# Half-head attention visits, a split last query chunk and a cross-chunk background order in a four-layer attention kernel

## The chip, the cores and the metric

One NeuronCore of a Trainium2 chip runs the whole program. The metric is the device time in microseconds (us) of one execution, from launch to the last output byte. Times of single instructions come from one profiled execution; its clock counts from the first instruction of the span.

The engines are named as in the profile: PE is TensorE (matmuls), PEld its weight loads, ACT is ScalarE (exponentials), DVE is VectorE, POOL is GpSimd, SP is SyncE, which issues the DMAs.

## The reference

Four layers, A, B, A, B, each a residual block around a layer norm. S is 2048 rows, D is 1024, 32 heads of 32. Layers 0 and 2 are linear attention with softmax features, layers 1 and 3 are full softmax attention (no mask).

```python
def _A_ref(x, wqkv, w_phi, wo):
    ...
    pq = jnp.einsum("bhsd,hdf->bhsf", q, w_phi)
    pk = jnp.einsum("bhsd,hdf->bhsf", k, w_phi)
    phi_q = jnp.concatenate([_softmax(pq, axis=-1), _softmax(-pq, axis=-1)], axis=-1)
    phi_k = jnp.concatenate([_softmax(pk, axis=-1), _softmax(-pk, axis=-1)], axis=-1)
    kv = jnp.einsum("bhsf,bhsd->bhfd", phi_k, v)
    z  = jnp.einsum("bhsf->bhf", phi_k)
    num = jnp.einsum("bhqf,bhfd->bhqd", phi_q, kv)
    den = jnp.einsum("bhqf,bhf->bhq", phi_q, z)[..., None] + 1e-6
    o = num / den
    return (lambda x, *d: x.transpose(*d))(o, 0, 2, 1, 3).reshape(B, S, D) @ wo
def _B_ref(x, wqkv, wo):
    ...
    scores = jnp.einsum("bhqd,bhkd->bhqk", q, k) * (Dh ** -0.5)
    p = _softmax(scores, axis=-1)
    o = jnp.einsum("bhqk,bhkd->bhqd", p, v)
    return (lambda x, *d: x.transpose(*d))(o, 0, 2, 1, 3).reshape(B, S, D) @ wo
...
x = x + _A_ref(_layernorm(x, axis=-1), A_wqkv, A_w_phi, A_wo)
x = x + _B_ref(_layernorm(x, axis=-1), B_wqkv, B_wo)
x = x + _A_ref(_layernorm(x, axis=-1), A_wqkv, A_w_phi, A_wo)
x = x + _B_ref(_layernorm(x, axis=-1), B_wqkv, B_wo)
```

## The kernel before

**Who sets the order.** The program is written by a small planner that runs while the kernel is built. `Clock` keeps a simulated time with a cost per operation (`c_act`, `c_ps`, `MM`, `DMA_LAT`); generators yield operations, tokens (`Slots`) and keys; what comes out is one fixed instruction list for each engine, and each engine then works through its list in order. The main loop (L1214 to L1251) first emits an attention step if one is ready, then sums, and otherwise picks a background piece.

**Attention (layers 1 and 3).** The rows are four chunks of 512. A unit is one pair of heads, one query chunk and a list of key chunks; the 16 pairs of one entry of `VISITS` (L194) make a visit, and visits go in the listed order, so that early query chunks start on the key chunks that exist. A step (`emit_step`) is 128 keys by two halves `e`: four row-tiled score matmuls of 512 columns into two `ring` tiles of PSUM, two exponentials of 128x1024 on ACT (L1098), and eight column-tiled matmuls of 512 columns (L1146 the values, L1150 the denominators) into the one `acc` bank. `finish_unit` copies `acc` to a block; a unit that is not the last for its queries stores it to `pd` in DRAM, and a later unit with `part` loads it back (`part_loader`) and adds. The last unit of a pair is normalised: its denominators go to DRAM and back in another shape (`dn`, `rc`), DVE takes the reciprocal, they go out again (`rn`), come back broadcast to 32 partitions each, and POOL multiplies into `oTB`. A `part` unit holds one of the 2 tokens `t_part` from its load to that product, and one of the 2 tokens `t_R` from the add on.

**Background.** All the rest is a list of tasks, here called pieces; each is up to 16 matmuls into one PSUM bank and a `post` that empties it. For a chunk c of a layer pair they are: `build_AQ` (8 query-feature projections `pq` with two exponentials each at L708, 4 denominators `ds`, 16 numerators `nn`, and a DMA transpose), `build_AO` (8 output projections with layer norm and DMA transpose behind), and `build_BP` (8 K, 8 Q and 8 V projections for the softmax layer). `build_AK` makes the linear layer's 8 feature pieces, 8 value pieces and 12 `kv` sums of a chunk; only when all four chunks are in does `kvm` exist. `build_BO` is the softmax layer's output projection, 8 pieces a chunk. The list's order is AQ, AO, BP for each chunk, and then BO for each chunk with AK of the next layer behind it.

**The bank.** `get_bank` gives out the one bank `bg_t`; only while no attention is active does it hand out halves of the `ring` as well. Outside attention the matmuls are whole 128x128 (L344), beside it they are split in four column tiles (L341). `pick` takes the first piece of a window of 24 whose keys are there.

**Tokens in a post.** The `post` of `pq` first asks for a token of `t_eq` (6 of them) and a block, and only then runs the two exponentials that empty the bank. The token comes back in `nn`:

```python
                n_cnt[l, c, gp] = n_cnt.get((l, c, gp), 0) + 1
                if n_cnt[l, c, gp] == 4:
                    for gi in range(2):
                        drop(t_eq, eq_b[l, c, 2 * gp + gi])
...
                n_cnt[l, c, gp] += 10
                if n_cnt[l, c, gp] == 44:
                    fq_s.give(f)
```

The first part runs when a piece's matmuls end and the second when its product has left the bank; the two tokens go back only if the count is exactly 4 at some point.

## Time and profile before

| what | value |
|---|---|
| median of 2 runs | 3058.73 us (3054.3 to 3063.15) |
| the profiled execution | 3048.71 us |
| its span, first to last instruction | 3046.9 us |
| PE busy, matmuls | 2480.4 us (81%) |
| ACT busy | 2079.3 us (68%) |
| DVE busy | 981.5 us (32%) |
| mean granted TensorE clock | 0.830 |

The profiled execution is 1.8 us longer than its span and 10 us under the median. A busy share is an average over stages that differ: between visits ACT does no exponentials at all, and within them it does little else, so stages are read one by one. PE's busy time counts pipelined matmuls and says little by itself.

### The profile page before, as it was taken

To read this page: it belongs to the slowest core of one execution; us is meant where nothing else is said; L and a number is where in the kernel's file an instruction comes from. 1 tells how busy PE (TensorE), PEld (TensorE's weight loads), DVE (VectorE), ACT (ScalarE), POOL (GpSimd) and SP (SyncE) were. 2 spreads that over 40 slices of the span, in tenths; PEclk is the share of its full clock that TensorE was granted. 3 is DMA by queue.
4 is the path that set the end of the run, shared out by engine and by line. 5 is a ranking of instruction groups with operands and counts; after the bars stand their busy time and mean duration, and the time that the engine had idled before them with its cause. 6 is when DMAs were issued, how large, how long until landed. Compare 5 with 4: busy or idle time off the path is not lost. (4 is left out here: it accounts for less than half of the span.)

```text
span 3046.9 us, 58388 instructions
## 1 busy us (share of the span) xinstructions
PE 2480.4 (81%) x23978; PEld 871.6 (29%) x23978; DVE 981.5 (32%) x1812; ACT 2079.3 (68%) x2387; POOL 295.6 (10%) x330
## 2 busy tenths in 40 slices
PE   5887888879878877669888787987988888866888
PEld 3443333233233122223213333322322322111212
DVE  5874342242042133434316534214213211111102
ACT  2442649929929878359992172993995688846996
POOL 0001100010011111111000101001001011111000
PEclk9998989689789689889968898976987977666767
DMA  5436453453144344433203555435322432222001
GB/s 180 111 111 184 142 157 113 134 154 116 46 123 121 94 120 124 127 124 87 88 28 107 163 167 152 133 121 164 103 79 74 124 99 78 79 80 69 28 21 34
DMA packets 356444, 332.06 MB, mean 109 GB/s; under 512 B 158296, under 2 KB 291416, under 8 KB 350800
## 3 DMA queue, kind: packets, MB, share of 16 engines
q1 hardware_dynamic: 356176, 328.33, 35.7%
q8 instruction: 187, 3.06, 0.4%
q14 instruction: 81, 0.66, 0.1%
HBM read 230.74 MB, written 72.32 MB: 99 GB/s over the span
## 5 line engine op out<-in xcount | busy, mean ns | idle before, releaser
L1098 ACT ACTIVATE E<-ring 128x1024 bf16<-128x1024 f32 x2048 | 1910.7, 1084 | 668.2 <-PE ring L1115 486.9
L1146 PE MATMUL acc<-E,V 128*32 128x512 bf16 x4096 | 775.4, 468 | 116.4 <-DVE blk L327 113.0
L1150 PE MATMUL acc<-E,ones 128*32 128x512 bf16 x4096 | 775.1, 468 | 0.0
L1115 PE MATMUL ring<-Q,K2b 32*128 32x512 bf16 x2048 | 472.8, 452 | 136.3 <-ACT E L1098 122.9
L1115 PE MATMUL ring<-Q,K2a 32*128 32x512 bf16 x2048 | 469.6, 455 | 15.7 <-ACT E L1098 11.4
L341 PE MATMUL bg<-xnT,slab 128*32 128x512 bf16 x4120 | 281.3, 387 | 26.1 <-DVE K2b L322 12.7
L1146 PEld LDWEIGHTS <-V 128*32 128x32 bf16 x4096 | 163.6, 102 | 465.5 <-issue 446.6
L942 DVE COPY blk<-acc 128x512 f32<-128x512 f32 x128 | 88.5, 691 | 633.5 <-PE acc L1150 630.3
L327 POOL TENSOR_TENSOR oTB<-blk,blk 64x512 bf16<-64x512 f32 x124 | 159.8, 1289 | 1104.4 <-DMA blk<-rn 1042.0
L1115 PEld LDWEIGHTS <-K2a 32*128 32x128 bf16 x2048 | 109.0, 93 | 533.0 <-issue 524.8
L1115 PEld LDWEIGHTS <-K2b 32*128 32x128 bf16 x2048 | 152.1, 93 | 303.6 <-issue 297.6
L327 POOL TENSOR_TENSOR blk<-blk 128x256 bf16<-128x256 f32 x128 | 91.6, 725 | 1227.4 <-DVE blk L327 1217.0
L327 DVE TENSOR_TENSOR blk<-blk,acc 128x512 f32<-128x512 f32 x128 | 87.8, 686 | 279.1 <-DMA blk<-pd 146.0
L341 PE MATMUL bg<-slab,xnT 128*32 128x512 bf16 x2220 | 159.2, 409 | 21.2 <-ACT blk L605 8.3
L1150 PEld LDWEIGHTS <-ones 128*32 128x32 bf16 x4096 | 154.6, 101 | 3.9
L341 PEld LDWEIGHTS <-slab 128*32 128x32 bf16 x4120 | 112.9, 98 | 148.5 <-issue 63.9
L344 PE MATMUL bg<-slab,xnT 128*128 128x512 bf16 x485 | 119.6, 389 | 27.5 <-DMA slab<-in_A_wqkv_dram 9.6
L344 PEld LDWEIGHTS <-xnT 128*128 128x128 bf16 x981 | 96.4, 99 | 157.6 <-issue 35.4
L963 DVE RECIPROCAL rc<-rc 128x8 f32<-128x8 f32 x124 | 24.9, 201 | 348.4 <-DMA rc<-dn 348.3
L344 PE MATMUL ring<-slab,xnT 128*128 128x512 bf16 x496 | 120.3, 384 | 7.5 <-ACT blk L605 4.1
L344 PE MATMUL bg<-xnT,slab 128*128 128x512 bf16 x226 | 68.0, 449 | 60.4 <-DMA xnT<-blk 52.0
L327 DVE TENSOR_TENSOR blk<-blk,bg 128x512 bf16<-128x512 bf16 x88 | 59.6, 677 | 151.1 <-PE bg L341 81.1
(98 smaller groups left out, 1846.5 us busy)
## 6 DMA issues: line engine op xcount, KB each, us to landing
slab<-in_B_wqkv_dram SPq DMA_DIRECT2D x48, 1024.0 KB
pd<-blk SPq DMA_DIRECT2D x128, 256.0 KB
blk<-pd SPq DMA_DIRECT2D x128, 256.0 KB
slab<-wf_pq SPq DMA_DIRECT2D x16, 1024.0 KB
slab<-in_A_wo_dram SPq DMA_DIRECT2D x16, 1024.0 KB
Q<-qd SPq DMA_DIRECT2D x128, 128.0 KB
Q<-qd SPq DMA_DIRECT2D x256, 64.0 KB
blk<-rn SPq DMA_DIRECT2D x248, 64.0 KB
```

What stands on the lines that cost most here:

```text
L327: return ("op", e, cost, lambda x: eng(x).tensor_tensor(out=o, in0=a, in1=b, op=op))
L341: nc.tensor.matmul(o[js], lhsT=l[:, js], rhs=r, start=st, stop=sp, tile_position=(0, 32 * j), skip_group_check=True)
L344: nc.tensor.matmul(o, lhsT=l, rhs=r, start=st, stop=sp, skip_group_check=True)
L942: yield ("op", "V", c_ps(512), lambda e: nc.vector.tensor_copy(out=a, in_=acc_t[:]))
L963: yield ("op", "V", 0.2, lambda e: nc.vector.reciprocal(out=rc[:], in_=rc[:]))
L1098: yield ("op", "S", c_act(1024), lambda x: nc.scalar.activation(out=E[:], in_=ring_t[buf][:], func=ACT.Exp, scale=INV_SQRT_DH))
L1115: nc.tensor.matmul(ring_t[bufs[e]][:, j, :], lhsT=K2[e][c][r, u.g, m, :], rhs=u.Q[r, e, :], start=True, stop=True, tile_position=(r0, 0), ...
L1146: nc.tensor.matmul(u.acc[n0 + 32 * j:n0 + 32 * j + 32, :], lhsT=Vc[c][:, kt, DH * h:DH * (h + 1)], rhs=E[:, j, :], start=first, stop=final ...
L1150: nc.tensor.matmul(u.acc[d0 + 32 * j:d0 + 32 * j + 32, :], lhsT=ones[:], rhs=E[:, j, :], start=first, stop=final, tile_position=(0, d0 + 3 ...
```

## The change

The softmax visits are split into halves of the heads (pairs 0 to 7, pairs 8 to 15), so that a visit needs only half the heads' K, Q and V; the last query chunk is visited as two halves of 256 rows (`w` is 2), whose steps take two key blocks at once so that an exponential stays 128x1024 and each matmul has 256 columns. `build_AQ` becomes `build_PQ` (the eight `pq`) and `build_DN` (`ds`, `nn`), `build_BP` works on one half of the heads, and the list mixes chunks. The output projection waits tile by tile. Feature, value and V pieces wait for their own tile of `xnT` (key `xt`) and not for four. A piece whose `post` needs a token now asks for token and block before it is picked (`pre`), and the two counts in `nn` are separate. Token counts: `t_eq` 6 to 8, `t_part` 2 to 4, `t_R` 2 to 3, `t_tmp` 2 to 3; blocks 22 to 23 (`phibd` now lies in `E0`); the window 24 to 60. `kvacc` serves as a third `xnT` buffer while it is free. The product's denominators take seven DMAs and not five (`rc` and `rn` in two parts each). Beside active attention the two exponentials of `pq` and `pk` are planned 0.5 us later (`ACT_SLACK`), and the planner's ACT cost is a little lower.

```diff
 class Turn:
...
+    def lend(self, limit, key):
+        self.limit, self.key = limit, key
+        self.give(self.extra)
...
 VISITS = (
-    (0, (0,), False, False),
-    (1, (0, 1), False, False),
-    (0, (1,), True, False),
-    (2, (0, 1, 2), False, False),
-    (0, (2, 3), True, True),
-    (1, (2, 3), True, True),
-    (2, (3,), True, True),
-    (3, (0, 1, 2, 3), False, True),
+    (0, 4, (0,), False, False, 0), (0, 4, (0,), False, False, 1),
+    (4, 4, (0, 1), False, False, 0), (0, 4, (1,), True, False, 0),
+    (4, 4, (0, 1), False, False, 1), (0, 4, (1,), True, False, 1),
+    (8, 4, (0, 1, 2), False, False, 0), (8, 4, (0, 1, 2), False, False, 1),
+    (0, 4, (2, 3), True, True, 0), (0, 4, (2, 3), True, True, 1),
+    (4, 4, (2, 3), True, True, 0), (4, 4, (2, 3), True, True, 1),
+    (8, 4, (3,), True, True, 0), (8, 4, (3,), True, True, 1),
+    (12, 2, (0, 1, 2, 3), False, True, 0), (12, 2, (0, 1, 2, 3), False, True, 1),
+    (14, 2, (0, 1, 2, 3), False, True, 0), (14, 2, (0, 1, 2, 3), False, True, 1),
 )
...
-    t_x, t_xn, t_phi, t_eq, t_o, t_oT = tok(4), tok(3), tok(8), tok(6), tok(4), tok(4)
-    t_q, t_acc, t_part, t_R, t_tmp = tok(2), tok(3), tok(2), tok(2), tok(2)
+    t_x, t_xn, t_phi, t_eq, t_o, t_oT = tok(4), tok(3), tok(8), tok(8), tok(4), tok(4)
+    t_q, t_acc, t_part, t_R, t_tmp = tok(2), tok(3), tok(4), tok(3), tok(3)
...
         drop(t_xn, xb2)
+        clk.set(("xt", u, tt_))
...
                 use_xn(u)
-                e = yield from grab(t_eq)
+                e = b
+                if att_active():
+                    yield ("sleep", ACT_SLACK)
...
-                n_cnt[l, c, gp] = n_cnt.get((l, c, gp), 0) + 1
-                if n_cnt[l, c, gp] == 4:
+                ke, kf = ("e", l, c, gp), ("f", l, c, gp)
+                n_cnt[ke] = n_cnt.get(ke, 0) + 1
+                if n_cnt[ke] == 4:
                     for gi in range(2):
                         drop(t_eq, eq_b[l, c, 2 * gp + gi])
-                tmp = yield from grab(t_tmp)
+                tmp = b
...
-                yield tt("P", c_pool(256),
+                yield tt("P" if att_active() else ("V", "P"), {"P": c_pool(256), "V": c_sb(256)},
...
-            yield dma(rc[:], dnd[i][:].rearrange("a (p e) -> (a p) e", e=8))
-            yield ("op", "V", 0.2, lambda e: nc.vector.reciprocal(out=rc[:], in_=rc[:]))
-            yield dma(rnd[i][:].rearrange("a (p e) -> (a p) e", e=8), rc[:])
+            for j in range(2):
+                yield ("op", "D", 0.07, lambda e, j=j: nc.sync.dma_start(
+                    out=rc[64 * j:64 * j + 64, 0:m], in_=dnd[i][j, 0:n].rearrange("(p e) -> p e", e=m)),
+                    DMA_LAT * j)
+            yield ("op", "V", 0.2, lambda e: nc.vector.reciprocal(out=rc[:, 0:m], in_=rc[:, 0:m]))
+            for j in range(2):
+                yield ("op", "D", 0.07, lambda e, j=j: nc.sync.dma_start(
+                    out=rnd[i][j, 0:n].rearrange("(p e) -> p e", e=m), in_=rc[64 * j:64 * j + 64, 0:m]),
+                    DMA_LAT * j)
...
-        for c in range(NC):
-            build_AQ(l, c)
-            build_AO(l, c)
-            build_BP(l + 1, c)
-        for q in range(NC):
-            build_BO(l + 1, q)
-            if l == 0:
-                build_AK(2, q)
+            build_PQ(0, 0)
+        b = l + 1
+        build_DN(l, 0)
+        build_PQ(l, 1)
+        build_AO(l, 0)
+        build_DN(l, 1)
+        build_BP(b, 0, 0)
+        build_AO(l, 1)
+        build_BP(b, 0, 1)
+        build_BP(b, 1, 0)
+        build_PQ(l, 2)
+        build_DN(l, 2)
+        build_BP(b, 1, 1)
+        build_AO(l, 2)
+        build_PQ(l, 3)
+        build_BP(b, 2, 0)
+        build_DN(l, 3)
+        build_BP(b, 2, 1)
+        build_AO(l, 3)
+        build_BP(b, 3, 0)
+        build_BP(b, 3, 1)
+        build_BO(b, 0, 4)
+        build_BO(b, 4, 8)
+        if l == 0:
+            build_AK(2, 0)
+        build_BO(b, 8, 12)
+        if l == 0:
+            build_AK(2, 1)
+            build_AK(2, 2)
+            build_PQ(2, 0)
+        build_BO(b, 12, 14)
+        if l == 0:
+            build_AK(2, 3, (0,))
+        build_BO(b, 14, 16)
+        if l == 0:
+            build_AK(2, 3, (1,))
...
+        for i, kk in enumerate(kks):
+            c, m = divmod(kk, 2)
+            for e in range(2):
+                for j in range(2):
+                    r0 = 64 * (e ^ u.b) + 32 * j
+                    r = slice(r0, r0 + 32)
+                    nc.tensor.matmul(
+                        ring_t[bufs[e]][:, j, i * n:(i + 1) * n], lhsT=K2[e][c][r, u.g, m, :],
+                        rhs=u.Q[r, e, 0:n],
+                        start=True, stop=True, tile_position=(r0, 0), skip_group_check=True)
+            st["t"] += MM * n / C
...
-                if clk.has(t.needs) and (t.slab is None or slab_ready.get(t.slab)):
+                if (clk.has(t.needs) and (t.slab is None or slab_ready.get(t.slab))
+                        and (t.pre is None or (t.pre.free and blk.free))):
                     b = get_bank()
                     if b is None:
                         return None
                     t.bank, t.rel = b
+                    if t.pre is not None:
+                        t.pre.take()
+                        t.b = blk.take()
...
-NBLK = 22
+NBLK = 23
+ACT_SLACK = 0.5
 NE = 5
-WINDOW = 24
+WINDOW = 60
```

## Rows read from the trace of the kernel before

**Rows 1.** Costliest group of ACT: busy us, mean ns, idle before and releasers.

```profile
L1098 ACT ACTIVATE E<-ring 128x1024 bf16<-128x1024 f32 x2048 | 1910.7, 1084 | 668.2 <-PE ring L1115 486.9 <-PE acc L1150 179.9
```

**Rows 2.** Stretches, attention exponentials (L1098) alone: us, ACT busy (x), PEclk, DMA, GB/s.

```profile
276.70:909.40 632.70, 417.91 (x449) 0.86 0.41 127
909.40:1607.90 698.50, 540.53 (x576) 0.84 0.34 101
1607.90:1744.70 136.80, 0.02 (x1) 0.86 0.50 142
1744.70:2384.00 639.30, 417.66 (x449) 0.85 0.41 126
2384.00:3023.40 639.40, 534.58 (x576) 0.71 0.23 66
3023.40:3046.90 23.50, 0.00 (x0) 0.86 0.12 45
```

**Rows 3.** The same view inside the first of them: first visit, and three gaps.

```profile
276.70:355.30 78.60, 60.30 (x64) 0.98 0.50 170
355.30:424.20 68.90, 0.02 (x1) 0.83 0.54 151
...
609.10:666.10 57.00, 0.01 (x1) 0.76 0.60 174
...
849.20:909.40 60.20, 0.07 (x1) 0.83 0.48 130
```

**Rows 4.** Background matmuls (L341) alone, two stretches: PE busy (x), PEld busy (x), PEclk, DMA.

```profile
909.40:990.00 80.60, 38.90 (x556) 15.32 (x548) 0.98 0.42 126
...
775.00:848.00 73.00, 0.00 (x0) 0.00 (x0) 0.72 0.11 39
```

**Rows 5.** ACT in order of time, query-feature exponentials: start, us, what.

```profile
756.18 0.61 ACT L708 ACTIVATE blk<-bg 128x512 bf16<-128x512 f32 x1
...
763.88 0.60 ACT L708 ACTIVATE blk<-bg 128x512 bf16<-128x512 f32 x1
...
848.96 0.66 ACT L708 ACTIVATE blk<-bg 128x512 bf16<-128x512 f32 x1
```

**Rows 6.** All engines in four stretches: PE, PEld, DVE, ACT, POOL busy (x), PEclk, DMA.

```profile
217.00:276.70 59.70, 42.06 (x248) 19.93 (x248) 32.67 (x67) 3.29 (x6) 13.68 (x20) 0.80 0.52 149
1607.90:1744.70 136.80, 104.96 (x577) 49.09 (x580) 84.81 (x153) 20.91 (x39) 15.81 (x24) 0.86 0.50 142
775.00:845.00 70.00, 60.87 (x466) 13.71 (x468) 4.14 (x6) 70.00 (x77) 0.00 (x0) 0.71 0.11 38
1451.00:1462.00 11.00, 9.73 (x108) 3.88 (x108) 3.78 (x8) 11.00 (x13) 0.09 (x1) 1.00 0.09 24
```

**Rows 7.** Late visits of query chunk 2 in both layers, L1098 alone, columns as in Rows 2.

```profile
1197.40:1344.50 147.10, 61.19 (x65) 0.87 0.48 143
...
2656.10:2778.90 122.80, 60.60 (x66) 0.61 0.29 84
```

**Rows 8.** SP in order of time through one part unit: start, us, what.

```profile
2612.34 0.35 SPq L309 DMA_DIRECT2D blk<-pd  x1
...
2615.72 0.50 SPq L309 DMA_DIRECT2D dn<-blk  x1
...
2625.19 0.38 SPq L966 DMA_DIRECT2D blk<-rn  x1
...
2628.64 0.38 SPq L309 DMA_DIRECT2D blk<-pd  x1
```

**Rows 9.** DVE and PE in order of time at the end: start, us, what.

```profile
3024.85 3.35 DVE L956 RECIPROCAL blk<-blk 64x512 f32<-64x512 f32 x1
...
3034.34 1.89 PE L344 MATMUL ring<-slab,oTB 128*128 128x512 bf16 x8
3036.07 1.89 PE L344 MATMUL bg<-slab,oTB 128*128 128x512 bf16 x8
```

**Rows 10.** Waits of PE: total us, times, longest.

```profile
PE bg L344 <- DMA xnT<-blk: 58.4, 8, 8.2
```

More of the change, by code (lines that the diff above doesn't have):

```diff
@@ L71, with __init__ @@
 class Turn:
-    def __init__(self, clk, items):
+    def __init__(self, clk, items, extra):
         self.clk = clk
         self.free = list(items)
+        self.extra = extra
         self.next = 0
         self.wait = {}
-    def _grant(self):
-        while self.free and self.next in self.wait:
+        self.limit = 0
+        self.key = None
+    def lend(self, limit, key):
+        self.limit, self.key = limit, key
+        self.give(self.extra)
+    def _grant(self):
+        while self.free:
+            if self.next >= self.limit and self.key and any(x is self.extra for x in self.free):
+                self.free = [x for x in self.free if x is not self.extra]
+                self.clk.set(self.key)
+                self.key = None
+                continue
+            if self.next not in self.wait:
+                return
             gen = self.wait.pop(self.next)
@@ L179, with __init__ @@
 class Task:
-    def __init__(self, name, needs, slab, mms, post):
+    def __init__(self, name, needs, slab, mms, post, pre=None):
         self.name = name
@@ L504, with add @@
     pinned = set()
-    def add(name, needs, slab, mms, post):
-        t = Task(name, needs, slab, mms, post)
+    def add(name, needs, slab, mms, post, pre=None):
+        t = Task(name, needs, slab, mms, post, pre)
         if slab is not None:
@@ L569, in post @@
                 else:
-                    b = yield from grab(t_tmp)
                     yield cp(b[:, 0:C], bank[:], C)
@@ L577, in post @@
                         clk.set(("wf", k))
-            add(f"fold{k}{m}", [("wT", k, g, m // 4) for g in range(4)], None, [one(g) for g in range(4)], post)
+            add(f"fold{k}{m}", [("wT", k, g, m // 4) for g in range(4)], None, [one(g) for g in range(4)], post,
+                t_tmp if k[0] == "pq" else None)
         for half in range(2):
@@ L655, in mms, with post @@
                 return o
-            def post(bank, rel):
+            def post(bank, rel, b):
                 for tg in tgs:
@@ L714, in pq, with build_DN @@
             add(f"pq{l}.{c}.{g}", [("xnT", u)], ("pq", g // 4),
-                mm8(lambda k, W: W[:, k, gl * P:(gl + 1) * P], lambda k, W: xn[u][:, k, :]), post)
+                mm8(lambda k, W: W[:, k, gl * P:(gl + 1) * P], lambda k, W: xn[u][:, k, :]), post, t_eq)
+        for g in range(G):
+            pq(g)
+    def build_DN(l, c):
         def kvm_keys(gp):
@@ L732, in ds, with post @@
                         mms.append((0.058, False, fn))
-            def post(bank, rel):
+            def post(bank, rel, b):
                 f = yield ("take", fq_s)
@@ L855, in qq, with post @@
             gl = g % 4
-            def post(bank, rel):
+            def post(bank, rel, b):
                 use_xn(u)
-                b = yield from grab(t_q)
                 yield cp(b[:, 0:C], bank[:], C)
@@ L1241 @@
                     slab_users[slab_of[t.slab]] -= 1
-                clk.start(t.post(t.bank, t.rel), st["t"] + 0.12)
+                clk.start(t.post(t.bank, t.rel, t.b), st["t"] + 0.12)
                 cur[0] = None
```

290 lines of the change are left out of this document (157 added, 133 removed).

## The prediction

> **What bounds the kernel now.** I read the costliest groups first. The 2048 attention exponentials are ACT's work: 1910.7 us busy of a span of 3046.9 [rows 1]. Where attention runs alone, 77 of them fill 70.00 us of 70.00, so one costs 0.91 us [rows 6]. That is the pace that nothing here changes; what can move is the time in which ACT has none to do. So the second view is that group alone, cut into stretches. The reader is to see six of them [rows 2]: a start of 276.7 us before the first exponential; a fill of layer 1 (632.7 us, of which 417.9 exponentials), in which chunks are still being projected; a finish of layer 1 (698.5, with 540.5); a transition of 136.8 with none; fill and finish of layer 3 (639.3 with 417.7, 639.4 with 534.6); a tail of 23.5.
>
> The third view cuts the fill. The first visit takes 78.6 us for 60.3 of exponentials, and three gaps of 68.9, 57.0 and 60.2 us hold none at all [rows 3]: there the next chunk is projected with nothing beside it. The fourth asks why it was not projected earlier. From 775 to 848 us not one background matmul ran, while attention went on [rows 4]. ACT shows the reason: query-feature exponentials come 7.7 us apart until 763.88, and the next is at 848.96, when the visit ends [rows 5]. That last piece held the only background bank all the while. The code says why its post can sit there: it asks for a `t_eq` token after it has the bank, and the count that gives tokens back misses the value 4 whenever one product ends before the fourth piece's post begins. Two lost tokens would leave four, and then a fifth projection stops the bank; that fits the four pieces before the gap. Such a stretch occurs four times, two in each layer, 264 us in all.
>
> The fifth view is one part unit on SP. Its load is issued at 2612.34, its denominators leave at 2615.72, come back broadcast at 2625.19, and the load that reuses its token is issued at 2628.64 [rows 8]. So a token is held 16.3 us, and two tokens allow a unit each 8.2 us. In the visits with one key chunk a unit has four exponentials, 3.6 us; 16 of them took 147.1 and 122.8 us for 61 of exponentials [rows 7].
>
> **The change, part by part.**
>
> *Fill.* Background pieces run at two paces. Beside attention 556 column matmuls, 17.4 pieces of 32, took 80.6 us, so 4.6 us each [rows 4]; a `pq` piece, which queues two exponentials behind attention's, takes about 7 (7.7 in the pair shown, [rows 5]). Alone, whole pieces start 1.73 us apart [rows 9]. `nn` pieces are not seen beside attention; `kv`, their likeness, went one per step there, 1.8 us, and ACT stayed full (11.00 of 11.00, [rows 6]). I walk the new list with these, 64 exponentials being 58 us.
> Wait 1, before the second half of the first visit: 8 AO pieces of chunk 1 and 6 of BP, 14 x 1.73 = 24 us. Wait 2, before chunk 1's first half: the 36 us just before cover 8 of 12 pieces, 4 x 1.73 = 7. Wait 3, before its second half: 87 us cover 6 BP (28) and 8 `pq` (56); DN 2 and 6 BP remain, about 20. Wait 4, before chunk 2: 87 us cover 6 BP, 8 AO (37) and 3 `pq`; 11 remain, 19. Waits 5 and 6: nearly covered, 2 each. Sum 74 us against 186 now [rows 3]. The fill becomes 417.9 + 18 (the slow first visit, which is limited by projections before and after) + 19 (16 `pq` of two 0.6 us exponentials, [rows 5]) + 74 = 529 us in each layer: 104 and 110 us less. Bounds: 25 us of waits if nearly all is covered, 130 if only the four stalls go (264 us are 57 pieces at 4.6, or 99 us at 1.73, half in each layer).
> Each half-visit adds Q loads (72 groups in a layer, not 64) on SP, at 0.3 to 0.6 us an issue like those of [rows 8]; SP has room here.
>
> *Moved queues.* DN pieces use the whole array and now stand between steps. The trace has such pieces beside attention, with ACT full and the clock at 1.00 [rows 6], so I add nothing. The Trainium skill, TensorEngine Tiling (Array Packing), section Tiling Modes, says that a change of tiling mode drains the TensorE; that speaks against this move. In that row PE idled 1.27 us over six such pieces, at most 0.21 each; for the 80 DN pieces of the fills the sum would be 17 us higher if the drains ended last.
>
> *Start.* PQ 1 and DN 1 now stand before the first softmax projections: 8 x 1.73 = 14 us on PE, and 16 products on DVE. PE idles 17.6 of the 59.7 us there and DVE 27 [rows 6]. Between 0 and 25 us; I take 8, since both have holes: 285. Tile-wise readiness could give some back.
>
> *Finish.* Four part tokens at 16.3 us would allow a unit each 4.1 us. Three R tokens, held from 2615 to 2629, allow 4.6. SP now issues, per part unit, one load, seven denominator DMAs and half of three Q loads, 9.5 x 0.42 = 4.0 us [rows 8]. So I take 4.5 us where ACT wants 3.6: 16 units, 14 us over ACT. The longer part units (7.3 us of exponentials) fall below ACT's pace. Layer 1: 540.5 + 44 (28 `pk` and 8 `pq` pieces, 1.2 us each) + 14 = 598, from 698.5. Layer 3: 534.6 + 14 = 549, from 639.4. Four stages of a token all behind SP is the weak point: at 6 us a unit it would be 24 us more in each layer.
>
> *Last chunk.* A step keeps its two exponentials but has 24 matmuls of 256 columns, not 12 of 512, the same columns. Not seen in the trace: the price of the three more groups of weight loads. From below 0 is the bound, as columns and exponentials do not fall; from above, 468 loads took 13.71 us, 0.12 us a group of four, so 0.35 us a step if none is hidden. PE is busy 60.87 of 70 there [rows 6], 1.58 of 1.82 us a step; 0.11 us would stick out, 28 us in 256 steps. I take 0, nearest to loads hidden as now.
>
> *Transition.* It loses 4 BO, 8 AK and 8 `pq` pieces, 20 x 1.73 = 35 us. But the shorter finish must take more: BO 110, three AK 342 (8 x 4.6 + 8 x 7 + 12 x 1.8 each, rounded), PQ 55, BO 18 and half an AK 57 make 582 us of pieces in some 475 after the first two visits. The 107 us over are 23 pieces, 40 us, in the transition. So 102 to 142; PE idles 32 us of it now [rows 6] and can take part of them: 118.
>
> *Tail.* 4 pieces fewer at 1.73, and a reciprocal of half the columns, 1.7 us of 3.35 [rows 9]: 23.5 - 6.9 - 1.7 = 15.
>
> Blocks go from 22 to 23 while tokens rise by ten; no wait for a block shows by name, so this stays a doubt inside the range.
>
> **The sum.** 285 + 529 + 598 + 118 + 529 + 549 + 15 = 2623 us of span, 1.8 more for the execution: 2625 against 3048.7. The median of the runs is 0.33% above the profiled execution, so 2633 us.
>
> **The rivals.**
> *Fill stays open.* The bank is freed but AO, DN and `pq` in front of the next half-visit keep ACT waiting: 130 us of waits in each layer, 2633 + 112 = 2745. For it: one bank, and the list puts DN 2 ahead of the projections that the visit needs. Against: the stalls are real and their cause is gone.
> *Finish bound by SP or blocks.* 6 us a unit, and a third of the longer visits' excess stays: 2 x (24 + 20) = 2721. For it: SP already waits in its order. Against: 4.0 us of issue is under 4.5.
> *Better overlap.* 25 us of waits in each layer and the transition at 102: 2633 - 98 - 16 = 2519. For it: DN pieces could use holes that my walk gives to nobody.
> *Last chunk bound by PE.* 2633 + 28 = 2661, up to 2720 if every load shows. The Trainium skill, TensorE: Matmul & The Clock Gate, Part 3, says that weight loads overlap running matmuls only where the row group differs; column tiles share theirs. Today's full ACT with 12 loads a step does not show it.
> *Slower than before.* In the fill PE reaches a piece whose transposed input has not landed, and the attention behind it in the same list waits. Now such waits stand in gaps: 8 of them, 58.4 us, 7.3 each [rows 10]. It decides from 430 us, 59 such waits inside attention; 67 make it 3120 us. Against: no background matmul beside attention (L341) shows such a wait.
>
> **How the numbers follow.** Forecast 0.56 (2550 to 2700), fill open 0.17, finish bound 0.08, better overlap 0.14, last chunk 0.03, slower 0.02. The range takes most of the open fill and half of the better case: 2520 to 2760. A measurement here tells about 2% from no change. All cases but the last lie over 2% below; some mixture may undo more than I see: faster 0.96, same 0.02, slower 0.02.
>
> **What would show it.** No stretch without background matmuls inside the fill; about 530 us from the first exponential to the first finishing visit; the visits of query chunk 2 with one key chunk near 72 us, with four part loads ahead; transition near 118, tail near 15. It is wrong if gaps of 50 us stay, if SP ends most waits of the late visits, or if steps of the last chunk exceed 1.85 us with ACT waiting for PE.

## The result, and the profile after

The changed kernel takes 2792.51 us (2789.08 to 2795.94, two runs) where the kernel before took 3058.73: a ratio of 0.913, with a 95% interval of 0.906 to 0.920. It is faster, as forecast, but 160 us over the forecast of 2633 and outside the range of 2520 to 2760. Its profiled execution took 2795.94 us, of which 2794.2 are the span.

First the view of [rows 2] for the kernel after: the attention exponentials alone (now at L1187), cut at the same six events.

```profile
0.00:289.40 289.40, 0.00 (x0) 0.96 0.49 144
289.40:808.40 519.00, 418.95 (x449) 0.96 0.49 147
808.40:1506.30 697.90, 547.98 (x577) 0.87 0.35 91
1506.30:1668.30 162.00, 0.05 (x2) 0.89 0.63 185
1668.30:2184.70 516.40, 418.94 (x449) 0.96 0.49 148
2184.70:2781.40 596.70, 534.72 (x577) 0.76 0.28 70
2781.40:2794.20 12.80, 0.00 (x0) 0.98 0.11 41
```

The whole miss can be read from it:

| stage | before | predicted | after | after - predicted |
|---|---|---|---|---|
| start | 276.7 | 285 | 289.4 | +4 |
| fill 1 | 632.7 | 529 | 519.0 | -10 |
| finish 1 | 698.5 | 598 | 697.9 | +100 |
| transition | 136.8 | 118 | 162.0 | +44 |
| fill 3 | 639.3 | 529 | 516.4 | -13 |
| finish 3 | 639.4 | 549 | 596.7 | +48 |
| tail | 23.5 | 15 | 12.8 | -2 |

The fills and the tail went as forecast. Finish 1 did not move at all, and the transition grew.

The same view inside fill 1, which answers to [rows 3]: the first visit's first half and the gaps ahead of the next ones, then (answering to [rows 7]) query chunk 2 with its last key chunk in layer 1 and layer 3, and last the second pair of two-tile visits of layer 3.

```profile
289.40:327.40 38.00, 29.86 (x32) 0.90 0.71 201
327.40:348.20 20.80, 0.01 (x1) 1.00 0.79 217
386.40:393.30 6.90, 0.00 (x1) 1.00 0.34 102
497.20:519.00 21.80, 0.00 (x0) 1.00 0.32 85
614.70:631.20 16.50, 0.03 (x1) 1.00 0.46 151
719.40:720.30 0.90, 0.03 (x1) 1.00 0.49 38
1097.70:1205.20 107.50, 62.25 (x66) 0.87 0.46 120
2434.90:2533.60 98.70, 60.77 (x66) 0.65 0.34 90
...
2662.60:2781.40 118.80, 118.33 (x129) 0.74 0.17 28
```

The gaps of 57 to 69 us are gone; those that remain are 20.8, 6.9, 21.8, 16.5 and 0.9 us (24, 7, 20, 19 and 2 had been walked out). The last line is the 256-column steps: 118.33 us of exponentials in 118.80, so they run at ACT's pace. The two lines of query chunk 2 are 6.7 and 6.2 us a unit, where 4.5 were forecast.

Who holds finish 1 shows in the waits of ACT and of SP's queue there: total us, times, longest.

```profile
ACT E L1187 <- PE ring L1207: 81.0, 56, 9.6
ACT E L1187 <- PE acc L1243: 50.6, 16, 17.0
...
SPq L1021 <- DMA rn<-rc: 63.4, 41, 7.2
SPq L1012 <- DMA dn<-blk: 58.3, 42, 5.5
SPq L1017 <- DMA rc<-dn: 27.5, 27, 3.7
```

ACT is short of 131.6 us of work there, in 72 waits, and the three largest sums of waits on SP's queue are for links of the denominators' round trip (`dn`, `rc`, `rn`): 149.2 us in 110 waits. SP works its list in order, so part loads, Q loads and the trips of other products stand behind each of these. In the first half visit of query chunk 2 in layer 3 SP has hardly a gap (in order of time, as in [rows 8]):

```profile
2443.41 0.59 SPq L333 DMA_DIRECT2D Q<-qd  x1
2444.05 0.50 SPq L333 DMA_DIRECT2D dn<-blk  x1
2444.64 0.34 SPq L333 DMA_DIRECT2D blk<-pd  x1
2445.10 1.12 SPq L1017 DMA_DIRECT2D rn<-rc  x2
2446.27 1.23 SPq L1012 DMA_DIRECT2D rc<-dn  x2
2447.60 0.49 SPq L333 DMA_DIRECT2D dn<-blk  x1
2448.19 0.33 SPq L1021 DMA_DIRECT2D blk<-rn  x1
...
2476.68 11.20 SPq L333 DMA_DIRECT2D out_dram<-blk  x3
2487.93 0.50 SPq L333 DMA_DIRECT2D dn<-blk  x1
```

The row of 11.20 us is three issues of 0.33 to 0.37 us and the waits between them: SP stands at the output blocks, and the next product's `dn` stands behind. From 2433.60 to 2476.57 such rows hold 68 issues, 37.6 us together, 0.55 us each. Six `dn`, 13 `rc` and 14 `rn` are among them, so the links of about seven products, one in some 6 us. Here the Trainium skill's page Perfetto Trace Analysis, section Optimizing DMA Performance, has the name for it: a kernel can be bound by the DMA sequencer, seen as an issuing queue that is solid DMA slices. This stretch agrees, 37.6 of 43.0 us; the two half visits together are less solid, 74.0 us of issues in 98.7. The same page's DMA Optimizations says that splitting DMAs into smaller ones may let some start sooner; the change splits two of them, and the run with them unsplit (below) shows that here it cost.

### The profile page after: what moved, and what is told of

The parts are those of the page before. It is cut to its first block, busy times and chain, and to the rows that moved or that the text cites. A ratio compares the mean times of both kernels' runs of the same rounds, so it can differ in the third digit from the quotient of the medians.

```text
span 2794.2 us, 67944 instructions
## 1 busy us (share of the span) xinstructions
PE 2321.4 (83%) x28313; PEld 922.3 (33%) x28313; DVE 977.9 (35%) x1885; ACT 2095.9 (75%) x2413; POOL 277.6 (10%) x327
## 5 line engine op out<-in xcount | busy, mean ns | idle before, releaser
L1187 ACT ACTIVATE E<-ring 128x1024 bf16<-128x1024 f32 x2048 | 1920.7, 1101 | 327.6 <-PE ring L1207 235.2
L1243 PE MATMUL acc<-E,V 128*32 128x512 bf16 (+1 forms) x5120 | 720.3, 385 | 82.8 <-DVE blk L351 68.4
L1243 PE MATMUL acc<-E,ones 128*32 128x512 bf16 (+1 forms) x5120 | 720.1, 385 | 0.0
L1207 PE MATMUL ring<-Q,K2b 32*128 32x512 bf16 (+1 forms) x2560 | 446.3, 376 | 149.8 <-ACT E L1187 143.4
L1207 PE MATMUL ring<-Q,K2a 32*128 32x512 bf16 (+1 forms) x2560 | 464.3, 377 | 39.9 <-DMA Q<-qd 27.2
L1243 PEld LDWEIGHTS <-V 128*32 128x32 bf16 x5120 | 212.8, 102 | 395.9 <-issue 364.8
L351 POOL TENSOR_TENSOR oTB<-blk,blk 64x512 bf16<-64x512 f32 (+1 forms) x156 | 167.0, 1071 | 1131.0 <-DMA blk<-rn 1042.8
L365 PE MATMUL bg<-xnT,slab 128*32 128x512 bf16 x2604 | 190.8, 414 | 28.0 <-ACT blk L758 9.7
L990 DVE COPY blk<-acc 128x512 f32<-128x512 f32 (+1 forms) x160 | 93.2, 582 | 268.3 <-PE acc L1243 266.4
L365 PE MATMUL bg<-kvacc,slab 128*32 128x512 bf16 x1580 | 109.0, 391 | 12.6 <-DVE K2b L346 9.3
L365 PE MATMUL bg<-slab,oTB 128*32 128x512 bf16 x1500 | 108.7, 413 | 10.0 <-DVE blk L351 8.9
```

The costliest lines, as they stand in the source:

```text
L351: return ("op", e, cost, lambda x: eng(x).tensor_tensor(out=o, in0=a, in1=b, op=op))
L365: nc.tensor.matmul(o[js], lhsT=l[:, js], rhs=r, start=st, stop=sp, tile_position=(0, 32 * j), skip_group_check=True)
L990: yield ("op", "V", c_ps(n), lambda e: nc.vector.tensor_copy(out=a, in_=acc_t[:, 0:n]))
L1187: yield ("op", "S", c_act(2 * n), lambda x: nc.scalar.activation(out=E[:, :, 0:n], in_=ring_t[buf][:, :, 0:n], func=ACT.Exp, scale=INV_SQR ...
L1207: nc.tensor.matmul(ring_t[bufs[e]][:, j, i * n:(i + 1) * n], lhsT=K2[e][c][r, u.g, m, :], rhs=u.Q[r, e, 0:n], start=True, stop=True, tile_ ...
L1243: nc.tensor.matmul(u.acc[r0 + 32 * j:r0 + 32 * j + 32, 0:n], lhsT=lh, rhs=E[:, j, i * n:(i + 1) * n], start=first, stop=final, tile_positi ...
```

## The experiments

All stages of all runs, from the same view (us). Fills that an edit leaves alone agree within 515 to 522, which is how far their stages can be compared. After has two runs, e11, e12, e15 and e16 have four, and every other variant has one. The kernel before, run beside each set, took 3038 to 3056 us. Runs of one kernel in one set differ by 5 to 16 us, so totals that lie as close decide nothing.

| run | time | start | fill 1 | finish 1 | transition | fill 3 | finish 3 | tail |
|---|---|---|---|---|---|---|---|---|
| before | 3058.7 | 277 | 633 | 698 | 137 | 639 | 639 | 24 |
| after | 2792.5 | 289 | 519 | 698 | 162 | 516 | 597 | 13 |
| e1 | 2827.8 | 287 | 515 | 706 | 164 | 515 | 626 | 13 |
| e2 | 2738.7 | 291 | 518 | 651 | 164 | 518 | 582 | 13 |
| e3 | 2775.6 | 290 | 519 | 662 | 161 | 519 | 600 | 23 |
| e4 (of before) | 2946.8 | 277 | 583 | 697 | 134 | 584 | 648 | 22 |
| e5 | 2774.1 | 281 | 518 | 687 | 157 | 518 | 599 | 13 |
| e6 | 2808.9 | 258 | 559 | 690 | 130 | 561 | 596 | 13 |
| e7 | 2700.1 | 287 | 517 | 611 | 174 | 521 | 575 | 13 |
| e8 | 2735.6 | 298 | 505 | 660 | 160 | 512 | 586 | 13 |
| e9 (of before) | 2919.4 | 278 | 636 | 643 | 132 | 635 | 573 | 22 |
| e10 | 2900.2 | 292 | 518 | 763 | 133 | 516 | 664 | 13 |
| e11 | 2690.8 | 295 | 511 | 613 | 171 | 512 | 572 | 13 |
| e12 | 2697.1 | 294 | 514 | 606 | 176 | 513 | 569 | 22 |
| e13 | 2778.7 | 291 | 517 | 678 | 167 | 521 | 590 | 13 |
| e14 | 2767.0 | 287 | 518 | 669 | 174 | 519 | 585 | 13 |
| e15 | 2669.3 | 284 | 521 | 602 | 171 | 519 | 562 | 13 |
| e16 | 2671.3 | 283 | 522 | 601 | 172 | 517 | 560 | 13 |
| e17 | 2726.2 | 286 | 518 | 637 | 161 | 516 | 584 | 22 |

**e1, the reciprocal on POOL.** DVE's reciprocal had waits of 264.0 us for `rc` in finish 1, with other DVE work behind it.

```diff
-            yield ("op", "V", 0.2, lambda e: nc.vector.reciprocal(out=rc[:, 0:m], in_=rc[:, 0:m]))
+            yield ("op", "P", 0.7, lambda e: nc.gpsimd.tensor_tensor(
+                out=rc[:, 0:m], in0=rc[:, 0:m], in1=neg1[:, 0:m], op=ALU.pow))
```

> The changed kernel with one edit: the reciprocal of the regrouped denominators (128x8) runs on POOL as a power of -1 and no longer on DVE. In the changed kernel DVE stands 264 us in the finish of layer 1 (697.9 us) and 309 us in that of layer 3 (596.7 us) in front of that reciprocal, waiting for the denominators' DMA, with the adds that free acc and the bank evacuations queued behind it. Theory 1 (DVE's place in its list is what stops PE and then ACT): finish of layer 1 near 630, of layer 3 near 565, whole near 2690. Rival (SP's issue is what is late, whoever takes the reciprocal): both finishes within 15 us of now, whole 2770 to 2800. Rival (POOL then waits instead, with layer norm behind it): layer 1's finish not shorter, transition longer, whole 2800 or more.

Slower, 2827.8. The wait moved with the instruction, to POOL's list in front of the multiplications, and the work grew: 1.42 us on the mean of both shapes, against 0.19 on DVE. Freeing DVE's list bought nothing: in finish 1 its adds then waited 84.0 us, and not 29.7, for part loads, which come through SP. As POOL now held the tokens longer, the run cannot say what a free DVE is worth by itself.

```profile
L1016 POOL TENSOR_TENSOR rc<-rc,neg 128x8 f32<-128x8 f32 (+1 forms) x156 | 220.9, 1416 | 353.1 <-DMA rc<-dn 350.7 <-POOL oTB L352 0.2
```

Waits of DVE in finish 1 (total us, times, longest), two of the kernel after and the last of e1:

```profile
DVE rc L1015 <- DMA rc<-dn: 264.0, 68, 12.3
DVE blk L351 <- DMA blk<-pd: 29.7, 9, 6.9
...
DVE blk L352 <- DMA blk<-pd: 84.0, 14, 13.1
```

**e2, five DMAs and not seven.** `rc` and `rn` move in one DMA each, as before the change (with scratch of their own for 256 columns).

```diff
-            for j in range(2):
-                yield ("op", "D", 0.07, lambda e, j=j: nc.sync.dma_start(
-                    out=rc[64 * j:64 * j + 64, 0:m], in_=dnd[i][j, 0:n].rearrange("(p e) -> p e", e=m)),
-                    DMA_LAT * j)
+            yield dma(rc[:, 0:m], dn_t[:].rearrange("a (p e) -> (a p) e", e=m))
...
```

> The changed kernel with the denominators' two regrouping DMAs back in one piece each (five DMAs for a product, not seven; for 256 columns a DRAM scratch of its own). It takes away 2 of some 9.5 SP issues of a part unit, at 0.33 to 0.6 us each. If SP's issue is the limit of the late visits: the visits of query chunk 2 with one key chunk fall from 107 and 98 us to 85 or less, layer 1's finish by 40 us or more, whole near 2730. If DVE's waiting place is the cause: the chain is about 1 us shorter, 15 us less in each finish, whole near 2760. If neither, 2785 to 2800.

2738.7: finish 1 falls by 47 us, finish 3 by 14, nothing else moves. The place was not as expected: the visits of query chunk 2 fell from 107 and 99 us to 100 and 92, not to 85, and 21 of the 47 us lie in the visits of the last chunk.

**e3, the last chunk whole.**

```diff
-    (12, 2, (0, 1, 2, 3), False, True, 0), (12, 2, (0, 1, 2, 3), False, True, 1),
-    (14, 2, (0, 1, 2, 3), False, True, 0), (14, 2, (0, 1, 2, 3), False, True, 1),
+    (12, 4, (0, 1, 2, 3), False, True, 0), (12, 4, (0, 1, 2, 3), False, True, 1),
```

> The changed kernel with the last query chunk in one piece of 512 rows (two half-head visits) instead of two of 256: half as many units and products there, matmuls of 512 columns. If the 256-column steps cost by themselves: the last chunk's visits, 301 us in layer 1 and 248 in layer 3, fall to about 264 and 240. If the products' DMAs cost: the same fall in layer 1, little in layer 3. The transition (162) should grow by the four output pieces and the eight feature and value pieces that then wait for the end, 20 to 30 us, the tail by 8. Whole 2770 to 2810.

2775.6: finish 1 falls by 36 us, finish 3 does not (+4), and the tail goes back to 23.1. The transition, which I expected to grow by 20 to 30 us, stays (161). The split pays in the tail and costs in layer 1.

**e4, before with the lost tokens returned.** Only the two counts in `nn` are kept apart; nothing else of the change.

```diff
...
-                n_cnt[l, c, gp] += 10
-                if n_cnt[l, c, gp] == 44:
+                n_cnt[kf] = n_cnt.get(kf, 0) + 1
+                if n_cnt[kf] == 4:
```

> The kernel before with one edit: the two counts in the numerators' post are kept apart, so that both feature tokens always come back. All else as before. If the four stretches of 264 us without background work come from lost tokens: they vanish, each layer's fill falls by 40 to 60 us, whole near 2945. If something else holds the bank: no change, 3040 to 3065. It tells how much of the fills' gain is this one repair and how much the new order.

2946.8. Fill 1 and fill 3 fall by 49 and 55 us, and the four stretches without background matmuls are gone from them. So under half of the fills' 114 and 123 us is the token repair. The rest belongs to the rest of the change, the new order and the halved visits above all; no run takes it apart.

**e5, V pieces behind their whole chunk.**

```diff
-            add(f"bv{l}.{c}.{t}.{h}", [("xt", u, t)], ("bv", h),
+            add(f"bv{l}.{c}.{t}.{h}", [("xnT", u)], ("bv", h),
```

> The changed kernel with one edit: a V piece waits again until its whole chunk of normalized x is transposed, as the K and Q pieces do, and not for its own tile alone. Theory: with the early readiness the V pieces run ahead of K and Q, so that the first Q is projected last and its trip through DRAM stands in front of the first visit (TensorE waits 6.7 us for it at the start and 6.3 us in the transition, where the kernel before had no such wait). Then the start falls from 289 to about 283 us and the transition from 162 to about 156, the fills stay at 519 and 516, and the whole is about 2780. Rival: the V pieces filled time in which nothing else could run, and without them the engine idles there and the V pieces follow the Q: start and transition stay within 2 us, or grow, and the whole is 2792 or more.

Start 280.9 (-8.5) and transition 156.6 (-5.4); e15 and e16, with the same edit, start at 284 and 283, and the runs that leave the start alone at 286 to 292. Finish 1 fell by 11 as well, which the theory does not explain. In the kernel after, the first scores of layer 3 wait for a Q that was projected last (SP's loads, then PE); in e5 V no longer goes ahead of it, and the longest wait of that kind is 2.6 us.

```profile
1664.15 0.57 SPq L958 DMA_DIRECT2D Q<-qd  x1
...
1667.64 0.61 PE L1207 MATMUL ring<-Q,K2a 32*128 32x512 bf16 x2 [6.33 <-DMA Q<-qd]
```

**e6, chunk 1's stages behind the first projections.**

```diff
         build_DN(l, 0)
-        build_PQ(l, 1)
         build_AO(l, 0)
-        build_DN(l, 1)
         build_BP(b, 0, 0)
+        build_PQ(l, 1)
+        build_DN(l, 1)
```

> The changed kernel with the order of the background stages at a layer's head changed: the first half of chunk 0's QKV projection goes in front of chunk 1's stages (DN0, AO0, first half of BP0, then PQ1, DN1), so that nothing of chunk 1 stands between the end of the kv sums and the first visit. Theory: the pieces of chunk 1 put there by the change are what the transition grew by beside the Q wait (from the last kv sum to the first exponential 90 us against 68 us before): transition from 162 to about 140, start from 289 to about 278, the wait in front of the second visit longer by some of that (7 to 10-20 us), whole about 2765. Rival: these pieces fill time in which the chain of chunk 0 (column sums, statistics, transposes) could not run faster, so that taking them out only opens gaps: start and transition fall by under 5 us each, the fills grow by 10 or more, whole 2792 or more.

Both theories were half right. Start and transition fall by 31 and 32 us, more than I said, and the fills grow by 40 and 45; the whole is 2808.9. The first four stages of e6:

```profile
0.00:258.50 258.50, 0.01 (x1) 0.94 0.50 149
258.50:817.50 559.00, 418.37 (x448) 0.95 0.49 149
817.50:1507.80 690.30, 546.66 (x577) 0.87 0.34 92
1507.80:1637.50 129.70, 0.00 (x0) 0.84 0.63 191
```

So the transition's growth is work moved into it; moved out again, this work costs the fills as much and about 10 us a layer more. The place in the list was right, and my price for it was not.

**e7, no denominators' DMAs.** All closing units take the path that the last two had.

```diff
-            if last and vi == len(VISITS) - 1:
-                units[-1].fast = units[-2].fast = True
+            if last:
+                for x in units[-8:]:
+                    x.fast = True
```

> The changed kernel with every finished product done as its last two are: the reciprocal on 64 lanes by VectorE at once (3.35 us for 512 columns, 1.75 for 256), and VectorE multiplies. The seven DMAs of the denominators' round trip (SP issues them in order, 0.3 to 0.6 us each, and waits in its queue) are gone, and 246 us of VectorE come in for each layer (48 times 3.84 us and 31 times 2.0 us), on an engine that was busy 214 us of the 698 in finish 1. Theory that SP's in-order queue sets the finish stages: finish 1 falls from 698 to below the 651 that five DMAs for seven gave, to about 625, finish 3 from 597 to about 570, whole about 2690. Rival, VectorE: a reciprocal of 3.35 us in front of the adds that free the banks of the sums takes the place of the wait for DMAs, finish 1 at 690 or more and finish 3 at 610 or more, whole 2800 or more.

2700.1. Finish 1 falls by 87 us, though DVE is now busy 443 of its 611 us and not 214 of 698; finish 3 falls by 22. The rival that DVE would take over fell. Finish 1 of the kernel after and of e7, busy times of PE, PEld, DVE, ACT and POOL:

```profile
808.40:1506.30 697.90, 543.53 (x8040) 217.59 (x8035) 213.97 (x405) 564.98 (x631) 91.24 (x90) 0.87 0.35 91
...
804.40:1415.00 610.60, 519.13 (x7856) 207.16 (x7849) 443.31 (x465) 556.33 (x625) 28.04 (x23) 0.92 0.27 84
```

**e8, SP's issues booked at 0.40 us.** The same DMAs, in another written order.

```diff
-        return ("op", "D", 0.07, lambda e: nc.sync.dma_start(out=o, in_=i), lat)
+        return ("op", "D", 0.40, lambda e: nc.sync.dma_start(out=o, in_=i), lat)
...
```

> The changed kernel with one figure of its planner changed: an issue on SP's queue is booked with 0.40 us (the trace shows 0.32 to 0.60) and not with 0.07. The same DMAs run; only the order in which all engines' instructions are written down can differ. Theory that SP lags its written order, and that TensorE waits because its own order was written for an SP that is never late: finish 1 falls from 698 to 650-680, finish 3 by 10-20, whole about 2745. Rival: it is the number of DMAs itself and not the order: both stages stay within 8 us, whole 2780 to 2800.

2735.6: finish 1 falls by 38 us and finish 3 by 10. A good part of SP's harm is that the other engines' lists were written for an SP that is never late.

**e9, before without the denominators' DMAs.**

```diff
-            if vi == len(VISITS) - 1:
-                units[-1].fast = units[-2].fast = True
+            if last:
+                for x in units[-16:]:
+                    x.fast = True
```

> The kernel before with one edit: all 64 finished products of a layer take VectorE's reciprocal on 64 lanes (3.35 us) and VectorE's multiplication, so that the seven DMAs of each are gone. Theory that the denominators' trip through SP's queue already bounded the finish of the kernel before: finish 1 falls from 698 to 650 or less, finish 3 from 639 to 600 or less, most of it in the visits of query chunk 2 (147 and 123 us), where two tokens are held for 16.3 us each, of which some 10 are that trip; whole about 2960. Rival: the trip was hidden before, and only the change put it on the path (16 more products, and half visits that close 4 units of four steps one after the other): finish 1 at 685 or more, finish 3 at 630 or more, whole 3030 or more. The fills should stay at 633 and 639 in both.

Finish 1 falls from 698 to 643 and finish 3 from 639 to 573, the fills stay. The trip, five DMAs here and not the seven of the expectation, already bounded the finish before the change. Not as expected: the gain is spread over all finishing visits (in layer 3 by 14, 16, 30 and 6 us), not mostly in query chunk 2.

**e10, part and R tokens undone.**

```diff
-    t_q, t_acc, t_part, t_R, t_tmp = tok(2), tok(3), tok(4), tok(3), tok(3)
+    t_q, t_acc, t_part, t_R, t_tmp = tok(2), tok(3), tok(2), tok(2), tok(3)
```

> The changed kernel with the tokens of the change undone: 2 for part loads and not 4, 2 for the broadcast reciprocals and not 3. Theory that SP's order and not the number of tokens sets a unit's time in the finish: the two half visits of query chunk 2 stay near 107 us in layer 1 and 99 in layer 3, finish 1 within 15 us of 698, finish 3 within 10 of 597, whole 2790 to 2815. Rival, as the prediction had it, that two tokens allow one unit each 8.2 us: the same visits go back to some 145 and 120 us, finish 1 up by 40, finish 3 by 20 to 25, whole about 2855.

The rival holds, and by more than it said: 2900.2, with the two finishes at

```profile
809.70:1572.70 763.00, 547.57 (x577) 0.87 0.34 96
...
2221.60:2885.70 664.10, 535.52 (x577) 0.71 0.24 64
```

So the tokens give 65 and 67 us, where the forecast took 100 and 90 off the two finishes by them. Without them the changed kernel's finish is 65 and 25 us worse than that of the kernel before: something else in the change took the gain back.

**e17, five DMAs and the last chunk whole** (the edits of e2 and e3 together).

> The changed kernel with both parts undone at once: five DMAs for the denominators of a product and not seven, and the last chunk whole. Theory that the two-tile visits cost by the 16 products more that go through SP's queue: then the two are one cost, and together they give about 60 us in finish 1 (not 83), 635 to 645, finish 3 at 580 to 588, the tail at 23, whole about 2735. Rival, that 256-column steps cost something of their own: the two add, finish 1 at 615 to 622, whole about 2715.

Finish 1 at 637, 61 us under the kernel after and not the 83 of the two by themselves: for the most part they are one cost, the queue's. These 61 us are close to the 65 that were taken back, though the 65 were measured with two tokens and the 61 with four. In layer 3 the two give 13 of 25; the other 12 I cannot assign.

**e11, e12, three edits.** e5, e7 and e8 together (e11), and the last chunk whole on top (e12).

> The changed kernel with three edits that each made it faster by itself: every product finished without the denominators' DMAs (2700), V pieces behind the whole chunk (2774), SP's issues booked with 0.40 us (2736). Theory that the first and the third treat the same thing, SP's in-order queue: together they give little over the first, finish 1 at about 605, and only the V pieces' 18 us come on top, whole 2670 to 2690. Rival, that the order is worth its 38 us beside it: finish 1 at 580 or less, whole 2650 or less.

> The same three edits, and the last query chunk whole again (two half-head visits of four query tiles). Theory that the two-tile visits cost by the 16 products more that they finish, each with its seven DMAs: without these DMAs the last chunk's 265 us in finish 1 fall by 10 or less and the tail's 10 us are lost, so the whole is within 10 us of the run before. Rival, that they cost by their 256-column steps and the more frequent change of banks, whatever the finish: the last chunk falls by 25 us or more in layer 1, and the whole is 15 us or more below the run before.

2690.8 (0.883 of before, 0.881 to 0.885) and 2697.1 (0.886, 0.884 to 0.888): the intervals overlap, and e12's tail is 9 us longer. Without the DMAs the better-written order is worth nothing (the finishes are those of e7), as it should be if both treat the same queue; the V pieces' gain at the start is lost too, and the order written with 0.40 us starts 9 us later by itself (e8: 298). And without the DMAs the whole last chunk is worth 7 us in finish 1, not 36.

**e13 to e16, buffers for normalized products.** In the kernel after and in every run with half visits so far but e10 (15 and 12 us), the first unit of query chunk 2's second half took 16 to 23 us where ACT wants 3.6. POOL's list in the kernel after shows why:

```profile
2461.13 1.26 POOL L351 TENSOR_TENSOR oTB<-blk,blk 64x512 bf16<-64x512 f32 x1 [3.29 <-DMA blk<-rn]
2485.36 3.82 POOL L351 TENSOR_TENSOR oTB<-blk,blk 64x512 bf16<-64x512 f32 x3 [22.97 <-PE bg L368]
```

Three multiplications stand 22.97 us behind a background matmul. There are 9 buffers `oTB`; a chunk fills 8, and all 8 come free only when its eight output projections are done, at 4.6 us each beside attention [rows 4], 37 us. A half visit of query chunk 2 is over sooner.

```diff
-    otb_s = Slots(clk, [sb(f"oTB{i}", [P, C]) for i in range(9)])
+    otb_s = Slots(clk, [sb(f"oTB{i}", [P, C]) for i in range(13)])
...
-NBLK = 23
+NBLK = 22
```

e13 has 11 buffers and all 23 blocks, e14 is the diff, e15 is the diff with e5 and e7, e16 has 15 buffers and 21 blocks.

> The changed kernel with 11 buffers for normalized products in place of 9, nothing else. Theory that a chunk's second group waits for the whole out-projection of the chunk before (8 pieces at 4.6 us, 37 us, against 29 us of exponentials in a half visit of query chunk 2): three groups, six units of 3.6 us, run ahead and not one, so the second half visit of query chunk 2 falls from 57.7 us in layer 3 to about 45 and from 64.4 in layer 1 to about 52, finish 3 from 597 to about 582, finish 1 from 698 to about 680, whole about 2760. Rival, that SP's queue and the part loads behind it hold these units: the same visits stay within 4 us, whole 2785 or more.

> The changed kernel with 13 buffers for normalized products, and 22 blocks in place of 23 to make room. Theory: five groups run ahead, which covers the 37 us of out-projection: the first unit of the second half visit of query chunk 2 takes 5 us or less and not 20, the first of the last chunk 9 or less and not 14 to 18; finish 3 at 570 to 578, finish 1 at 660 to 675, whole about 2745. Rival, blocks: one block fewer gives back what the buffers bring, whole within 10 us of the run with 11.

> 13 buffers and 22 blocks, every product finished without the denominators' DMAs, and V pieces behind their whole chunk; SP booked as in the changed kernel. Theory that SP's trip and these buffers are two separate limits which together make the finish's excess: finish 1 at about 580 and finish 3 at about 548 (the prediction had 598 and 549), the transition still 165 to 175 because a shorter finish takes less of the background, whole about 2640. Rival, that VectorE (4.7 us a unit beside its background work, where ACT wants 3.6) holds the units of query chunk 2 once the buffers are there: its two half visits stay at 90 us or more in layer 1, whole 2670 or more.

> The same with 15 buffers and 21 blocks. Theory that 13 already cover the out-projection: within 8 us of the run with 13. Rival: in layer 1 the pieces of layer 2 stand between those of the out-projection, so that it takes longer than 37 us there: finish 1 lower by 10 or more, whole 10 us lower or more.

With 11 the long first unit is already gone (4 us in both layers, from 21 and 20), but only the second half visit of layer 3 falls, to 52 us; that of layer 1 stays at 64, where 52 had been expected. With 13 it falls to 56, and finish 1 and 3 fall by 29 and 12 us: a limit of its own; finish 1 is as expected, finish 3 7 us above its upper end. In layer 1 the transition takes 12 of the 29 back. e15 and e16 are the fastest kernels. e15 took 2669.3 us, 0.876 of before (0.873 to 0.878), 4.4% under the change alone. e16 is the same within its interval (0.874 to 0.879), so 13 are enough. But e15 missed the 2640 it was expected at, and its rival's signs came, at the edge: query chunk 2 in layer 1 took 93 us, where 90 were to show DVE as the holder, and the whole 2669, where it said 2670. DVE is all but full in these visits (89.21 of 93.00 us in layer 1). The two finishes of e15 (attention exponentials), then all engines in query chunk 2 of layer 3, where DVE is busy 75.16 of 79.50 us:

```profile
804.50:1406.50 602.00, 542.38 (x577) 0.93 0.28 84
2095.60:2657.50 561.90, 532.57 (x577) 0.78 0.19 58
...
2338.50:2418.00 79.50, 66.93 (x625) 19.96 (x618) 75.16 (x54) 60.28 (x65) 0.00 (x0) 0.74 0.32 98
```

## Why the prediction was right, and where it failed

**Fill: right.** 519 and 516 against 529. Both causes named there are real; e4 splits them, 49 and 55 us for the lost tokens, 64 and 68 for the rest of the change. The DN pieces between attention steps cost nothing that shows. The rule of the Trainium skill weighed there (TensorEngine Tiling (Array Packing), Tiling Modes: a change of mode drains the engine) would have made each fill 17 us longer if it ended last; with the fills 10 and 13 us under the forecast, this trace gives no sign of that.

**Last chunk's matmuls: right at nothing.** 256-column steps keep ACT full (118.33 of 118.80 us). But "a step keeps its two exponentials" looked only at steps: the split also makes 16 more closing products in a layer, each with its trip through SP. That is most of the 36 us of e3 (without the trip 7 of them are left, e12 beside e11), and I priced it at zero.

**Finish: the step that failed** is "SP now issues ... 9.5 x 0.42 = 4.0 us ... So I take 4.5 us", and with it "The longer part units (7.3 us of exponentials) fall below ACT's pace". The tokens do what the prediction says (e10, 65 and 67 us). SP's price was wrong in size and in kind: I took the queue as a rate, and it works in order. The number of issues was about right: in the trace the half visits of query chunk 2, 16 units in a layer, hold 146 issues in layer 1 and 143 in layer 3, nine a unit. But they kept SP busy 82.2 of 107.4 and 74.0 of 98.6 us, 5.1 and 4.6 us a unit and not 4.0. The unit itself cost 6.7 and 6.2 us, because the queue also stands still. One such stop is not the trip's: ACT's gap of 17 and 16 us before the second half visit, over a third of these visits' excess over ACT's pace, is that of the `oTB` buffers, which I had not looked at; more buffers shortened the visits by 8 and 10 us (e14).

More important is where the rest lies. The visits of query chunk 2 are 35 and 27 us over the 72 forecast. The other 65 of finish 1 and 21 of finish 3 are in units that I held safe. The half visits of query chunk 1 in layer 1, 60.64 and 61.20 us of exponentials, took 74.9 and 77.0 us, and SP's issues filled only 49.6 and 40.5 us of that, while links of the trip held the head of its queue for 36.6 us in the two. There the order counts for more than the rate. e8 bears this out: the same DMAs in another written order give 38 us of finish 1 back.

My rival *Finish bound by SP* had its 6 us a unit, but only 0.08 of the chance, and 88 us in both layers where 148 were due. Taking the trip away gives 87 of the 100 us in finish 1 and 22 of the 48 in finish 3. Of the rest, 9 and 13 us more go in e15 with the `oTB` buffers (and, in finish 1, perhaps with the V pieces, which e15 moves too). e15 then has 602 and 562 where I forecast 598 and 549, but in layer 1 that is partly luck: I had added 44 us for feature pieces on ACT in finish 1, and ACT's whole other work there was 17 us (564.98 less 547.98). So the forecast was 27 us too high for another reason, which hid as much of the miss.

**Transition: failed in two steps.** I priced PQ 1 and DN 1 at the start (8 us) and forgot that the same list stands at the head of layer 3. e6 puts these pieces at 32 us in the transition and 31 at the start. And the last sums of layer 2's keys ended 75 us after the last exponential of layer 1, as long as before (72), where I had taken 35 us of pieces out and let the shorter finish put 16 back. These two rows are the last key products, of the kernel after and of the one before.

```profile
1581.28 0.41 DVE L351 TENSOR_TENSOR kvm<-kvacc,J 128x256 bf16<-128x256 f32 x1
```

```profile
1678.34 1.35 DVE L327 TENSOR_TENSOR kvm<-kvacc,J 128x384 bf16<-128x384 f32 x3
```

That a shorter finish leaves more to the transition is borne out at the ends: it was 133 us beside a finish of 763 (e10), 162 beside 698 and 174 beside 611 (e7). Between them it is no rule: 161 beside 637 (e17), 174 beside 669 (e14).

**Start: near, by luck.** Two errors go the same way: I took 8 us for what cost 31 (e6), and tile-wise readiness, which "could give some back", cost 8.5 by putting V ahead of Q (e5). The start grew by 12.7 us and not by 39.5, so something else in the change gave back some 27, and no run isolates it.

**Tail: right.** DVE's last reciprocal took 1.75 us for 256 columns, against 3.35 [rows 9].

```profile
2782.58 1.75 DVE L1004 RECIPROCAL blk<-blk 64x256 f32<-64x256 f32 x1
```

**Open.** In layer 3, 12 of the 25 us that the change costs the finish without its tokens. In e15, finish 3 keeps 13 us over the forecast, and finish 1 is as long as forecast though the forecast had 27 us too much. The half visits of query chunk 2 take 93.0 and 79.5 us there where 72 were forecast, with DVE busy 89.21 and 75.16 of them, so DVE is the likely holder of that part, but no run takes work from it to show it.

## What to carry to other kernels

A queue that works in order is not priced by issues times time alone: measure the time of an issue where the queue is dense, count what waits at its head, and give each extra buffer or token only the gain that the next shared queue leaves. When a change splits work, count everything that happens once per piece (here the closing of a product, with seven DMAs), not only the steps. And follow a freed resource back to who really frees it: a buffer returned by a background piece ties the critical path to the background's pace.

## What the hardware showed that I had not expected

A reciprocal of 512 columns on 64 lanes, 3.35 us of DVE, is far cheaper here than the trip that avoids it, whose arithmetic is 0.19 us: in e7 DVE is busy 1455.5 us in all and not 977.9, 239 us more in each layer, and the kernel gains 92 us. A power of -1 on POOL took 1.65 us for 128x8 and 1.04 for 128x4. And PE, with steps of 256 columns and twice the matmul count, kept ACT at 118.33 of 118.80 us.
